# A third group turned by VectorE and the DMA queue, and four sums in an earlier step

## The chip, the cores and the metric

The kernel runs on one core of a Trainium2 chip. The core has TensorE (PE: matrix products and transposes through an identity), VectorE (DVE), ScalarE (ACT), GpSimd (POOL) and SyncE (SP), whose queue issues most of the DMA transfers. Each engine takes its instructions in order and waits on semaphores for the others. The metric is the device time of one execution in microseconds. Before the change the median of three executions is 694.56 us (694.55 to 695.29).

## The reference

The input `u` is a sequence of 2048 rows with 512 channels. The first half of the work, A, is a state-space convolution with a skip term; the second, B, is a mixer with two MLPs.

```
h   = u + A(layernorm(u))
x   = layernorm(h)
g   = gelu(layernorm(x) @ w1)                  # 512 -> 512, layer 1
x1  = x + shifted(g) @ w2                      # four channel quarters shifted by +1, -1, +2, -2 rows; layer 2
h2  = gelu(layernorm(x1) @ w3) @ w4            # 512 -> 1792 -> 512, layers 3 and 4
out = h + x1 + h2
```

All is float32. The products of B are made from split operands: each operand is written as a high part (fp32r) and the rest (low part), and three products of them are summed.

## The kernel before

The convolution (`conv_phase`) takes the first 300 us and is not touched. `mixer_phase` works on the 2048 rows as sixteen tiles of 128 rows, in four groups `q` of four tiles; the order of the groups is 3, 0, 1, 2. For each group `norm1(q)` writes the normalized rows into one of four large tiles `XQ[0]` to `XQ[3]` (128x2048); group 2 uses `XQ[0]`. `turn1(q)` makes the transposed operand `XT[q]` of layer 1: sixteen TensorE transposes of 128x128 into four PSUM banks, then for each of four chunks of channels a cast on ScalarE (high part) and a subtraction on VectorE (low part). `layer1(q, f)` is twelve matmuls of 128x512 for each quarter `f` of the outputs, and a gelu on ScalarE with a low part on VectorE. `layer2(j)` is twelve matmuls for one tile, whose result VectorE adds to the residual into the tile `X1[q]`; for tiles below 8 GpSimd adds it to `h` and VectorE takes the statistics for the second norm.

The products of layers 1 to 4 share four PSUM banks in rotation (pool `ps2`, rows named `l` or `l3a` to `l3g` in the profile), so a matmul group has to wait until the group four places earlier has been read.

Layer 3 is done for two halves of the rows (pair 0 and pair 1), each in seven steps, so that `s` runs from 0 to 13; a step makes seven products with operand sums in the manner of Strassen's scheme. Its operands are the turned tiles of `x1` (`FT[q, c]`), their sums t1 to t4 (`sums2`), and the high and low parts of them all (`halve`; `fresh` for pair 1). In a step, `layer3a` makes the products a, b, c and e, with VectorE adding them up; then comes the fourth layer of the step before (`layer4a`), then `layer3b` with f, d, g and the gelus, then `layer4b`. `turn2(q)` turns a group of `x1` without TensorE: VectorE transposes 32x32 blocks of the whole tile into a second `XQ` tile, four instructions in all, and sixteen DMA transfers of 32x512 from SP's queue put the blocks in their places.

The list `todo` holds small pieces of work, and `some(n)` issues the next `n` of them at the place in the program where it is called; `some(4)` stands at the end of each step.

The order of instructions on each engine is the order in which the code is written; `InOrder` keeps it, and every instruction made through it has line 87 in the profile, so groups of instructions are told apart by the names of their tiles. The order around the change is the list of calls in lines 1424 to 1431 and the loop over `s` from line 1543:

```
    norm1(2), sum3(), layer1(1, 0), layer1(1, 1), layer1(1, 2), turn1(2), layer1(1, 3), load3(0), raw3(1)
    layer2(2), layer2(3), norm2(0), layer2(4), layer2(5)
    layer1(2, 0), turn2(0), layer1(2, 1), load4(0), raw4(1), layer1(2, 2), sum3(), layer1(2, 3), layer2(6)
...
        if s == 4:
            turn2(3)
        if s == 5:
            todo.extend(sums2(1, 0) + sums2(1, 1)), some(4)
```

`raw3` and `raw4` issue the loads of the next weights on SP, `sum3` adds weight quarters on GpSimd, `load3` and `load4` split the weights on ScalarE and GpSimd, and `norm2(q)` normalizes a group of `x1` in place.

Of the kernel before, what the change touches and what calls it, by code (L numbers as in the profile page):

```python
# [11 lines left out]
F32 = mybir.dt.float32  # L12
# [3 lines left out]
ALU = mybir.AluOpType  # L16
# [1112 lines left out]
def mixer_phase(ctx, tc, cst, h, out, finish, w3, w4):  # L1129

    nc = InOrder(tc)
# [10 lines left out]
    def slab(name):  # L1142
        return sl.tile([128, 512], F32R, tag="slab", name=name)

    def slot(i):
        return cst["slab"](i)
# [4 lines left out]
    XQ = [w1p.tile([128, 4 * 512], F32, name=f"xq{i}") for i in range(4)]  # L1151
    X1 = {0: XQ[3], 1: XQ[1], 2: XQ[2], 3: XQ[0]}
    quarter = lambda t, i: t[:, i * 512 : i * 512 + 512]
    turned = lambda t: t.rearrange("p (a c x) -> p c a x", a=4, c=4)
    natural = lambda t: t.rearrange("p (i a t) -> p i a t", i=4, a=4)
# [56 lines left out]
    H1, XL, XT = {}, {}, {}  # L1212

    def norm1(q):
        XL[q] = []
        for j in range(q * 4, q * 4 + 4):
            t = quarter(XQ[{3: 0, 0: 1, 1: 2, 2: 0}[q]], j % 4)
            if (q == 0 and j % 2) or (q == 3 and j != 14):
                nc.vector.tensor_scalar(t, h[:, j, :], mv[:, j, 0:1], r12[:, j : j + 1], ALU.subtract, ALU.mult)
            else:  # L1220
                nc.scalar.activation(t, h[:, j, :], AF.Identity, scale=r12[:, j : j + 1], bias=off12[:, j : j + 1])
            XL[q].append(t)

    def turn1(q):
        XT[q] = transposed(XL.pop(q), f"xt{q}", 2 if q == 3 else 0)

    def layer1(q, f):
        b = bank(f"l1_{q}_{f}")
        n = 0
        seq = [(c, wi, xi) for c in range(4) for wi, xi in PROD]  # L1230
        if (q, f) == (3, 0):

            seq.sort(key=lambda k: 2 * k[0] + 3 * k[2])
        for c, wi, xi in seq:
            nc.tensor.matmul(b, W1[f][wi][:, c * 128 : c * 128 + 128], XT[q][c][xi], start=(n == 0), stop=(n == 11))
            n += 1
        H1[q, f] = gelu(b, f"h1_{q}_{f}")

        tiles = {0: ((15, 0),), 2: ((14, 1), (15, 2)), 1: ((0, 3),), 3: ((0, 4), (1, 5))}[f]
        for t, i in tiles:  # L1240
            if t // 4 != q:
                continue
            for k in range(2):
                src = H1[q, f][k][:, t % 4 * 128 : t % 4 * 128 + 128]
                dst = wrap[k][i // 4][:, i % 4, :]
                if f in (0, 2):
                    nc.gpsimd.tensor_copy(dst[:, 32:128], src[:, 0:96].bitcast(F32))
                    nc.gpsimd.tensor_copy(dst[:, 1:32], src[:, 96:127].bitcast(F32))
                    nc.gpsimd.tensor_copy(dst[:, 0:1], zero)
                else:  # L1250
                    nc.gpsimd.tensor_copy(dst[:, 0:96], src[:, 32:128].bitcast(F32))
                    nc.gpsimd.tensor_copy(dst[:, 96:127], src[:, 1:32].bitcast(F32))
                    nc.gpsimd.tensor_copy(dst[:, 127:128], zero)
# [11 lines left out]
    def layer2(j):  # L1265
        q, i = divmod(j, 4)
        b = bank(f"l2_{j}")
        n = 0
        for f, sh in enumerate((-1, 1, -2, 2)):
            for wi, xi in PROD:  # L1270
                nc.tensor.matmul(b, h1_block(f, j + sh, xi), W2[f][wi], start=(n == 0), stop=(n == 11))
                n += 1
        x1 = quarter(X1[q], i)
        nc.vector.scalar_tensor_tensor(x1, h[:, j, :], r1[:, j : j + 1], b, ALU.mult, ALU.add)
        xq[j] = x1
        if j < 8:
            residual(j), stats2(j)
# [27 lines left out]
    def norm2(q):  # L1305
        for op in norm2_ops(q):
            op()
# [4 lines left out]
    FT, XC, W3, W4 = {}, {}, {}, {}  # L1312

    def turn2(q):

        x, t = X1[q], XQ[{0: 2, 2: 3, 3: 1}[q]]
        blocks = t.rearrange("p (b c i t) -> p i c b t", b=4, c=4, i=4)
        for i in range(4):
            nc.vector.transpose(blocks[:, i], quarter(x, i).rearrange("p (c b t) -> p c b t", c=4, b=4))
        for a in range(4):  # L1320
            for b in range(4):
                nc.sync.dma_start(quarter(x, a)[b * 32 : b * 32 + 32], quarter(t, b)[a * 32 : a * 32 + 32])
        for c in range(4):
            FT[q, c] = turned(x)[:, c]

    def turn2_wide(q):

# [11 lines left out]

    def halve(src, pair, name, c, low=nc.vector):  # L1340

        hi, lo = slab(f"{name}{pair}{c}h"), slab(f"{name}{pair}{c}l")
        src = src.rearrange("p a (i t) -> p i a t", i=4)
        nc.scalar.copy(natural(hi), src)
        low.tensor_tensor(natural(lo), src, natural(hi).bitcast(F32), ALU.subtract)
        XC[pair, name, c] = hi, lo

    def sums2(pair, c):

# [11 lines left out]
    todo = []  # L1361

    def some(n):
        while n and todo:
            todo.pop(0)()
            n -= 1
# [5 lines left out]
    def raw3(s):  # L1372
        f = s % half
        for i in range(2):
            o = (f + i * half) * 128
            nc.sync.dma_start(raw["ab"[i]].rearrange("p (c f) -> p c f", c=4),
                              w3[:, o : o + 128].rearrange("(c p) f -> p c f", p=128))

    def sum3():
        a11, a12, a21, a22 = (raw[n][:, i * 256 : i * 256 + 256] for n in "ab" for i in range(2))  # L1380
        s1, s2, s3, s4 = (raw["s"][:, i * 256 : i * 256 + 256] for i in range(4))
        nc.gpsimd.tensor_tensor(s1, a21, a22, ALU.add)
        nc.gpsimd.tensor_tensor(s3, a11, a21, ALU.subtract)
        nc.gpsimd.tensor_tensor(s2, s1, a11, ALU.subtract)
        nc.gpsimd.tensor_tensor(s4, a12, s2, ALU.subtract)

    def load3(s, low=nc.gpsimd, parts=range(3)):
        ra, a22, sm_ = raw["a"], raw["b"][:, 256:512], raw["s"]
        if s % 2:
            one, four, last = (slot(11), slot(14)), (slots(9, 2), slots(12, 2)), slot(8)  # L1390
        else:
            one, four, last = (slot(20), W3S[0]), (slots(16, 2), slots(18, 2)), W3S[1]
        for i, (src, (hi, lo)) in enumerate(((ra, one), (sm_, four), (a22, (last[:, 0:256], last[:, 256:512])))):
            if i not in parts:
                continue
            nc.scalar.copy(hi, src)
            low.tensor_tensor(lo, src, hi.bitcast(F32), ALU.subtract)
        at_ = lambda w, i: w[:, i * 256 : i * 256 + 256]
        W3[s] = dict(a11=[at_(w, 0) for w in one], a12=[at_(w, 1) for w in one], a22=[at_(last, i) for i in range(2)],
                     **{f"s{i + 1}": [at_(w, i) for w in four] for i in range(4)})  # L1400
# [23 lines left out]
    norm1(3), finish(0, early), turn1(3), gelus(), finish(0, late), root([0]), norm1(0)  # L1424
    layer1(3, 0), layer1(3, 1), layer1(3, 2), turn1(0), finish(1), root([1]), layer1(3, 3), norm1(1), raw3(0), raw4(0)
    finish(2, early), layer1(0, 0), layer1(0, 1), layer1(0, 2), layer1(0, 3), turn1(1), finish(2, late), root([2]), layer2(0), layer2(1)
    norm1(2), sum3(), layer1(1, 0), layer1(1, 1), layer1(1, 2), turn1(2), layer1(1, 3), load3(0), raw3(1)
    layer2(2), layer2(3), norm2(0), layer2(4), layer2(5)
    layer1(2, 0), turn2(0), layer1(2, 1), load4(0), raw4(1), layer1(2, 2), sum3(), layer1(2, 3), layer2(6)
    layer2(7), norm2(1)  # L1430
    for n in ("b11", "b21"):
# [111 lines left out]
    for s in range(2 * half):  # L1543
        turn, last = s + 1 == half, s + 1 == 2 * half
        layer3a(s)
        if turn:
            fresh(("b11", "t2", "t3", "t1"))
        if last:
            load4(s)
        else:  # L1550
            load3(s + 1, *((nc.gpsimd,) if s else (nc.vector, range(1, 3))))
        if s + 2 < 2 * half:
            raw3(s + 2)
        if s:
            layer4a(s - 1)
        if s == 1:
            for j in range(8, 12):
                residual(j), stats2(j)
        if s == 2:
            for j in range(12, 16):  # L1560
                stats2(j)
            norm2(2)
            for j in range(12, 16):
                residual(j)
        if s == 3:
            turn2(2), norm2(3)
        if s == 4:
            turn2(3)
        if s == 5:
            todo.extend(sums2(1, 0) + sums2(1, 1)), some(4)  # L1570
        late = layer3b(s)
        if not last and s:
            load4(s), raw4(s + 1)
        if s + 2 < 2 * half:
            sum3()
        if s:
            layer4b(s - 1, late)
        else:
            late()
        some(4)  # L1580
        if turn:
            fresh(("b21", "t4", "b22"))
# [45 lines left out]
```

## Time and profile before

| | |
|---|---|
| median of three runs | 694.56 us (694.55 to 695.29) |
| the profiled execution | 695.48 us |
| its span, first to last instruction | 693.4 us |
| mean granted TensorE clock | 0.995 |
| TensorE matmul busy | 656.0 us, 95% of the span |
| VectorE, ScalarE, GpSimd busy | 538.6, 411.2, 397.8 us |

A row of the timeline gives the start, the duration, the engine, the line, the operation, the tile written and the tiles read with their shapes, the number of instructions merged into the row, and in brackets the idle time before it and what ended that. Buffer numbers are left out of the names: `l` is any PSUM bank of layers 1, 2 and 4, `u` any of a step's four accumulators, `xt` the PSUM banks of the transposes. Matmuls are pipelined: the next one starts before the end that a row gives.

### The profile page before, as it was taken

Reading aid. Unit: us, or ns where it says so; the run is one execution under the profiler, and the core shown is the slowest. Engines: PE = TensorE matmul, PEld = TensorE weight load, DVE = VectorE, ACT = ScalarE, POOL = GpSimd, SP = SyncE. Lnnn points to the kernel's source line nnn. Section 1 sums busy time; section 2 is a strip of 40 time slices with the busy share of each in tenths; the row PEclk is TensorE's granted clock in tenths of the full one; section 3 lists DMA queues with packets and bytes.
Section 4 is the critical chain, followed back from the end, with each engine's and each line's share of the span. In section 5 each row is a group of like instructions: output and inputs, shape, how many; then the busy total and the mean of one; then the engine's idle time right before and its main releaser. Section 6 shows DMA issues by size and latency. Waiting matters only on the chain.

```text
span 693.4 us, 16766 instructions
## 1 busy us (share of the span) xinstructions
PE 656.0 (95%) x6854; PEld 511.8 (74%) x6854; DVE 538.6 (78%) x946; ACT 411.2 (59%) x712; POOL 397.8 (57%) x406
## 2 busy tenths in 40 slices
PE   5887999998999998989999999999999999999997
PEld 5884756663676674848888888888887888888886
DVE  5998998999898998987776799766679954554544
ACT  7889878867799974236643455445445543444330
POOL 1889589967999998002555309455534655553310
PEclk9998999999999999999999999999999999999999
DMA  8830654010301132010012011223411352211004
GB/s 216 258 140 2 186 160 102 3 48 32 64 2 49 34 108 93 2 61 1 1 32 72 20 30 32 61 83 99 114 40 31 105 140 61 61 46 45 17 15 122
DMA packets 47216, 48.34 MB, mean 70 GB/s; under 512 B 5668, under 2 KB 32292, under 8 KB 47140
## 3 DMA queue, kind: packets, MB, share of 16 engines
q1 hardware_dynamic: 46372, 46.22, 23.2%
q10 hardware_dynamic: 768, 1.05, 0.6%
q8 instruction: 54, 0.88, 0.5%
q14 instruction: 22, 0.18, 0.1%
HBM read 35.72 MB, written 8.39 MB: 64 GB/s over the span
## 4 chain that ended last, share of the span: by engine, by line
PE 58%; DVE 19%; ACT 12%; issue 4%; POOL 4%; DMA 2%; SPq 1%; DVEq 0%; ACTq 0%; POOLq 0%
PE l L87 24%; PE acc L87 10%; ACT pt L87 7%; PE bank L87 6%; DVE u L87 5%; DVE at L87 3%; DVE cs L87 3%; DVE sn L87 3%; PE l3c L87 3%; PE l3f L87 3%; PE l3e L87 3%; PE l3a L87 2%; PE l3b L87 2%; PE l3g L87 2%; PE l3d L87 2%
## 5 line engine op out<-in xcount | busy, mean ns | idle before, releaser
L87 ACT ACTIVATE pt<-pt 128x1056 f32<-128x1056 int32 x64 | 69.9, 1092 | 14.3 <-DVE cs L87 6.6
L87 POOL TENSOR_TENSOR pt<-p,s 128x512 int32<-128x512 int32 x64 | 72.0, 1143 | 5.1 <-DVE sn L87 4.1
L87 PE MATMUL bank<-at,tbs 128*64 128x128 f32 (+1 forms) x768 | 63.1, 311 | 3.4 <-DVE u L87 1.6
L87 PEld LDWEIGHTS bank<-at,tbs 128*64 128x64 f32 x768 | 44.5, 134 | 20.8 <-ACT at L87 3.0
L87 PEld LDWEIGHTS bank<-ident 128*128 128x128 f32 x418 | 50.5, 198 | 8.3 <-issue 5.1
L87 PE MATMUL bank<-ident 128*128 128x128 f32 x418 | 54.6, 287 | 0.0
L87 PE MATMUL bank<-u,ms 64*128 64x128 f32 x768 | 50.5, 280 | 3.5 <-DVE at L87 1.3
L87 PEld LDWEIGHTS bank<-u,ms 64*128 64x128 f32 x768 | 45.3, 187 | 8.2 <-issue 1.8
L87 POOL TENSOR_TENSOR cs0w<-raw,cs0w 128x512 fp32r<-128x512 f32 x7 | 9.4, 1346 | 62.4 <-ACT cs0w L87 50.1
L87 DVE TENSOR_TENSOR cs<-pt,amx 128x512 f32<-128x512 f32 x64 | 40.9, 677 | 2.5 <-ACT pt L87 1.3
L87 DVE TENSOR_TENSOR h<-h,l 128x512 f32<-128x512 f32 x48 | 32.3, 686 | 12.0 <-PE l L87 12.0
L87 DVE TENSOR_TENSOR u<-u,l3f 128x512 f32<-128x512 f32 x14 | 9.6, 686 | 40.5 <-PE l3f L87 40.5
L87 PEld LDWEIGHTS bank<-cs 128*32 128x32 f32 x1024 | 24.1, 111 | 23.0 <-POOL cs L87 6.0
L87 PE MATMUL bank<-cs 128*32 128x64 f32 x1024 | 32.4, 224 | 9.1 <-DVE cs L87 4.8
L87 POOL TENSOR_TENSOR cs1w<-raw,cs1w 128x512 fp32r<-128x512 f32 x7 | 9.5, 1362 | 52.9 <-ACT cs1w L87 39.5
L87 ACT COPY at<-bank 128x512 f32<-128x512 f32 x40 | 24.9, 630 | 22.9 <-PE bank L87 22.8
L87 ACT ACTIVATE pt<-pt,halfpi 128x1056 f32<-128x1056 f32 x32 | 38.1, 1191 | 0.5
L87 POOL TENSOR_TENSOR sn<-pt,amp 128x512 f32<-128x512 f32 x30 | 36.9, 1229 | 1.4 <-ACT pt L87 1.0
L87 DVE STREAM_TRANSPOSE at<-bank 128x512 f32<-128x512 f32 (+1 forms) x40 | 35.6, 919 | 1.5 <-PE bank L87 1.5
L87 ACT ACTIVATE u<-u 128x512 f32<-128x512 f32 x56 | 35.4, 633 | 1.8
L87 PE MATMUL bank<-sn 128*32 128x64 f32 x1024 | 31.9, 222 | 2.6 <-DVE sn L87 2.5
L87 POOL TENSOR_TENSOR cs<-pt,amp 128x512 f32<-128x512 f32 x26 | 31.9, 1227 | 3.4 <-PE bank L87 1.1
(1163 smaller groups left out, 2080.6 us busy)
## 6 DMA issues: line engine op xcount, KB each, us to landing
raw<-in_B_w_dram SPq DMA_DIRECT2D x28, 256.0 KB, 2.7
h<-in_A_u_dram SPq DMA_DIRECT2D x32, 128.0 KB, 4.2
h<-in_A_u_dram SPq DMA_DIRECT2D x16, 256.0 KB, 4.1
rawa<-in_B_w_dram SPq DMA_DIRECT2D x14, 256.0 KB, 2.9
rawb<-in_B_w_dram SPq DMA_DIRECT2D x14, 256.0 KB, 2.7
ms<-in_mm_dram SPq DMA_DIRECT2D x4, 768.0 KB, 11.1
xq<-xq SPq DMA_DIRECT2D x48, 64.0 KB, 2.0
out_dram<-h SPq DMA_DIRECT2D x48, 64.0 KB, 1.7
```

Of the source, the lines that this page charges most:

```text
L87: ins = f(*args, **kw)
```

## The change

The code of `turn2` becomes a function `swap(x, t)`, and that of `halve` a function `parts(src, name, low)`; `turn2` and `halve` call them and do what they did. New is that `turn1(2)` is gone. In its place `swap(XQ[0], XQ[1])` is called right after `norm1(2)` and `sum3()`, ahead of `layer1(1, 0)`, and the four chunks are split by `parts` after `layer2(3)`, ahead of `norm2(0)`. Operand sums of pair 1: the first four, `sums2(1, 0)`, are put on the list in step 4 and so are issued at its end; the other four, `sums2(1, 1)`, are issued in the middle of step 5, where the first four were.

```diff
+    def swap(x, t):
+
+        blocks = t.rearrange("p (b c i t) -> p i c b t", b=4, c=4, i=4)
+        for i in range(4):
+            nc.vector.transpose(blocks[:, i], quarter(x, i).rearrange("p (c b t) -> p c b t", c=4, b=4))
+        for a in range(4):
+            for b in range(4):
+                nc.sync.dma_start(quarter(x, a)[b * 32 : b * 32 + 32], quarter(t, b)[a * 32 : a * 32 + 32])
+        return [turned(x)[:, c] for c in range(4)]
+
+    def parts(src, name, low=nc.vector):
+
+        hi, lo = slab(f"{name}h"), slab(f"{name}l")
+        src = src.rearrange("p a (i t) -> p i a t", i=4)
+        nc.scalar.copy(natural(hi), src)
+        low.tensor_tensor(natural(lo), src, natural(hi).bitcast(F32), ALU.subtract)
+        return hi, lo
...
-    norm1(2), sum3(), layer1(1, 0), layer1(1, 1), layer1(1, 2), turn1(2), layer1(1, 3), load3(0), raw3(1)
-    layer2(2), layer2(3), norm2(0), layer2(4), layer2(5)
+    norm1(2), sum3()
+    third = swap(XQ[0], XQ[1])
+    layer1(1, 0), layer1(1, 1), layer1(1, 2), layer1(1, 3), load3(0), raw3(1)
+    layer2(2), layer2(3)
+    XT[2] = [parts(v, f"xt2{c}") for c, v in enumerate(third)]
+    norm2(0), layer2(4), layer2(5)
...
         if s == 4:
-            turn2(3)
+            turn2(3), todo.extend(sums2(1, 0))
         if s == 5:
-            todo.extend(sums2(1, 0) + sums2(1, 1)), some(4)
+            todo.extend(sums2(1, 1)), some(4)
```

What stands on TensorE between the third and the last quarter of group 1's first layer, before (`xt2_0` to `xt2_3` are the PSUM banks of the transposes, `xq0` is `XQ[0]`):

```order
L87 MATMUL l1_1_2_4419<-xt13l_4317,cs1w_3641 128x512
L87 MATMUL l1_1_2_4419<-xt13h_4316,cs1w_3641 128x512
L87 MATMUL xt2_0_4438<-ident_61,xq0_3948 128x128 x4
L87 MATMUL xt2_1_4439<-ident_61,xq0_3948 128x128 x4
L87 MATMUL xt2_2_4440<-ident_61,xq0_3948 128x128 x4
L87 MATMUL xt2_3_4441<-ident_61,xq0_3948 128x128 x4
L87 MATMUL l1_1_3_4474<-xt10h_4292,sn0w_3588 128x512
```

And after; the last quarter follows at once:

```order
L87 MATMUL l1_1_2_4439<-xt13l_4317,cs1w_3641 128x512
L87 MATMUL l1_1_2_4439<-xt13h_4316,cs1w_3641 128x512
L87 MATMUL l1_1_3_4458<-xt10h_4292,sn0w_3588 128x512
L87 MATMUL l1_1_3_4458<-xt10l_4293,sn0w_3588 128x512
L87 MATMUL l1_1_3_4458<-xt10h_4292,sn0w_3588 128x512
```

On VectorE at the same place, before (`h1_1_0l` to `h1_1_3l` are low parts of group 1's gelus, `xt20l` to `xt23l` those of the turned third group):

```order
L87 BN_AGGR mv2_0_4351<-st1_1_4370 128x2
L87 TENSOR_TENSOR h1_1_0l_4395<-gh1_1_0_4396,h1_1_0h_4394 128x512
L87 TENSOR_TENSOR h1_1_1l_4414<-gh1_1_1_4415,h1_1_1h_4413 128x512
L87 TENSOR_TENSOR h1_1_2l_4433<-gh1_1_2_4434,h1_1_2h_4432 128x512
L87 TENSOR_TENSOR xt20l_4447<-xt2_0_4438,xt20h_4446 128x512
L87 TENSOR_TENSOR xt21l_4455<-xt2_1_4439,xt21h_4454 128x512
L87 TENSOR_TENSOR xt22l_4463<-xt2_2_4440,xt22h_4462 128x512
L87 TENSOR_TENSOR xt23l_4471<-xt2_3_4441,xt23h_4470 128x512
L87 TENSOR_TENSOR h1_1_3l_4488<-gh1_1_3_4489,h1_1_3h_4487 128x512
L87 SCALAR_TENSOR_TENSOR xq3_3951<-h_66,rr_67,l2_2_4501 128x512
```

And after, where the block transposes stand ahead of the gelus' low parts, and those of the third group (not in these rows) behind the sums and statistics of `layer2(2)` and `layer2(3)`, with `XQ[0]` as their source:

```order
L87 BN_AGGR mv2_0_4351<-st1_1_4370 128x2
L87 STREAM_TRANSPOSE xq1_3949<-xq0_3948 128x4x4x32 x4
L87 TENSOR_TENSOR h1_1_0l_4415<-gh1_1_0_4416,h1_1_0h_4414 128x512
L87 TENSOR_TENSOR h1_1_1l_4434<-gh1_1_1_4435,h1_1_1h_4433 128x512
L87 TENSOR_TENSOR h1_1_2l_4453<-gh1_1_2_4454,h1_1_2h_4452 128x512
L87 TENSOR_TENSOR h1_1_3l_4472<-gh1_1_3_4473,h1_1_3h_4471 128x512
L87 SCALAR_TENSOR_TENSOR xq3_3951<-h_66,rr_67,l2_2_4485 128x512
```

The casts of the third group move in the same way on ScalarE, behind the weights of `load3(0)` and ahead of `norm2(0)`. On SP the sixteen transfers stand ahead of `raw3(1)`.

On VectorE from the end of step 4 into step 5, before (`u_5` are step 5's accumulators, `xq` the tiles that hold the operands and sums of pair 1):

```order
L87 TENSOR_TENSOR h<-h,l_3_3_5779 128x512
L87 TENSOR_TENSOR u_5_5788<-u_5_5787,l3b_5799 128x512
L87 TENSOR_TENSOR u_5_5789<-u_5_5788,l3c_5807 128x512
L87 TENSOR_TENSOR u_5_5790<-u_5_5789,l3e_5815 128x512
L87 TENSOR_TENSOR u_5_5788<-u_5_5788,l3e_5815 128x512
L87 TENSOR_TENSOR xq_3951<-xq_3948,xq_3950 128x512
L87 TENSOR_TENSOR xq_3948<-xq_3948 128x4x128
L87 TENSOR_TENSOR xq_3951<-xq_3948,xq_3951 128x512
L87 TENSOR_TENSOR xq_3951<-xq_3950,xq_3951 128x512
L87 TENSOR_TENSOR u_5_5787<-u_5_5787,l3f_5864 128x512
```

And after; the same four sums stand ahead of the first addition of step 5, and the four of the second chunk (into `xq_3949`) where these were. At the end of step 5 no sum is left:

```order
L87 TENSOR_TENSOR h<-h,l_3_3_5779 128x512
L87 TENSOR_TENSOR xq_3951<-xq_3948,xq_3950 128x512
L87 TENSOR_TENSOR xq_3948<-xq_3948 128x4x128
L87 TENSOR_TENSOR xq_3951<-xq_3948,xq_3951 128x512
L87 TENSOR_TENSOR xq_3951<-xq_3950,xq_3951 128x512
L87 TENSOR_TENSOR u_5_5792<-u_5_5791,l3b_5803 128x512
L87 TENSOR_TENSOR u_5_5793<-u_5_5792,l3c_5811 128x512
L87 TENSOR_TENSOR u_5_5794<-u_5_5793,l3e_5819 128x512
L87 TENSOR_TENSOR u_5_5792<-u_5_5792,l3e_5819 128x512
L87 TENSOR_TENSOR xq_3949<-xq_3948,xq_3950 128x512
```

More of the change, by code (lines that the diff above doesn't have):

```diff
@@ L1314, in turn2 @@
     def turn2(q):
[L1316 to L1324, printed above, removed]
+        for c, v in enumerate(swap(X1[q], XQ[{0: 2, 2: 3, 3: 1}[q]])):
+            FT[q, c] = v
     def turn2_wide(q):
@@ L1340, in halve @@
     def halve(src, pair, name, c, low=nc.vector):
[L1342 to L1346, printed above, removed]
+        XC[pair, name, c] = parts(src, f"{name}{pair}{c}", low)
     def sums2(pair, c):
```

## The prediction

> **What bounds the kernel now.** I read the page's busy shares first, then the stretches around the two places that the change touches, then TensorE's waits in them, then the single instructions there.
>
> ```profile
> PE 656.0 (95%) x6854; PEld 511.8 (74%) x6854; DVE 538.6 (78%) x946; ACT 411.2 (59%) x712; POOL 397.8 (57%) x406
> ```
>
> The share is an average, so the stretches matter more (from:to, length, then busy time of PE, PEld, DVE, ACT, POOL, PE clock, DMA):
>
> ```profile
> 342.00:373.00 31.00, 31.00 (x147) 25.85 (x146) 20.23 (x40) 15.91 (x30) 18.27 (x15) 1.00 0.10 26
> 373.00:513.00 140.00, 139.93 (x623) 115.22 (x622) 103.28 (x187) 67.89 (x113) 65.78 (x59) 1.00 0.22 63
> 513.00:532.00 19.00, 18.54 (x82) 15.04 (x81) 18.05 (x21) 8.68 (x16) 9.92 (x8) 1.00 0.18 56
> 532.00:689.20 157.20, 157.20 (x694) 129.78 (x692) 90.46 (x131) 64.78 (x108) 65.89 (x58) 1.00 0.23 64
> ```
>
> From 342 us to the last matmul TensorE is busy without a break at clock 1.00, but for about half a microsecond before 532. The table of waits has one line for it in that time:
>
> ```profile
> PE l L87 <- DVE u L87: 0.5, 1, 0.5
> ```
>
> So in the whole second phase a microsecond taken from TensorE's queue is a microsecond of the kernel, as long as nobody else becomes late. Work on VectorE, ScalarE and the queues costs nothing until TensorE has to wait for it.
>
> **First part: the transposes of the third group.** TensorE's rows there:
>
> ```profile
> 346.22 0.40 PE L87 MATMUL l<-xt13h,cs1w 128*128 128x512 f32 x1
> 346.45 1.91 PE L87 MATMUL xt<-ident,xq 128*128 128x128 f32 x16
> ...
> 348.43 0.39 PE L87 MATMUL l<-xt10l,sn0w 128*128 128x512 f32 x1
> ...
> 361.87 0.39 PE L87 MATMUL l<-xt20h,cs0w 128*128 128x512 f32 x1
> ```
>
> A row's length is longer than its turn: the step from 346.22 to 346.45 shows that one wide matmul takes 0.23 us of the queue. Without the sixteen transposes the first matmul of layer1(1, 3) starts at 346.45 and the second at 346.68, where now it starts at 348.43: 1.75 us gained. Everything behind moves up by that, so layer1(2, 0), which first needs the third group, wants it at 361.87 - 1.75 = 360.1.
>
> What must be ready then takes a long way round. Its links, on ScalarE, VectorE, the DMA queue and ScalarE again (the 366 and 369 rows are the same swap of group 0, which this kernel already does, and the last two give the pitch of a cast from such a tile):
>
> ```profile
> 339.78 2.94 ACT L87 ACTIVATE xq<-h,rn,rr 128x512 f32<-128x512 f32 x4 [4.95 <-DVE rn L87]
> ```
> ```profile
> 342.74 0.18 DVE L87 BATCH_NORM_AGGREGATE mv<-st 128x2 f32<-128x6 f32 x1
> ...
> 347.77 0.69 DVE L87 TENSOR_TENSOR h_2l<-gh,h_2h 128x512 fp32r<-128x512 f32 x1 [2.03 <-ACT gh L87]
> ...
> 358.36 0.17 DVE L87 TENSOR_SCALAR qa<-mv 128x4 f32<-128x4 f32 x1
> ...
> 361.40 0.74 DVE L87 SCALAR_TENSOR_TENSOR xq<-h,rr,l 128x512 f32<-128x512 f32 x1
> ...
> 366.59 2.48 DVE L87 STREAM_TRANSPOSE xq<-xq 128x512 f32<-128x512 f32 x4
> ```
> ```profile
> 369.15 10.14 SPq L1322 DMA_DIRECT2D xq<-xq  x16
> ```
> ```profile
> DMA to landing us min/median/max: 1.9/2.0/2.6
> ```
> ```profile
> 385.06 0.61 ACT L87 CAST b1100h<-xq 128x512 fp32r<-128x512 f32 x1
> 385.57 0.61 ACT L87 CAST b1101h<-xq 128x512 fp32r<-128x512 f32 x1
> ```
>
> The normalized group is written by 339.78 + 2.94 = 342.7 and VectorE is free at 342.74 + 0.18 = 342.9. Four block transposes take 2.48: 345.4. SP has nothing else in front of the sixteen transfers; their issue takes 10.14, from 345.5 to 355.6, the last one starting at about 355.0 and landing 2.0 to 2.6 later: 357.0 to 357.6. Every chunk of the turned tile takes rows from all quarters, so ScalarE's first cast waits for the last transfer. Four casts at a pitch of 0.51 run from 357.1; the first is done at 357.7. The first VectorE subtraction then ends at about 358.4, and with a pitch of 0.60 (the rows of t1 in the chain below) the fourth at 360.3.
>
> TensorE wants the first high part at 360.1 (slack 2.4 us), the first low part one matmul later at 360.3 (slack 1.9), the fourth low part ten matmuls later at 362.4 (slack 2.1). So by these rows the whole detour is hidden, and a slip above 1.9 us starts to cost TensorE one for one.
>
> What stands behind the moved instructions: VectorE is held 2.5 us more before the low parts of layer1(1, 0) and (1, 1), which then run from 345.4 to 346.7; the third, at 347.77, is not touched. ScalarE and VectorE both wait at the third group until 357 to 358; behind them are norm2(0) and, on VectorE, the residual sum of layer2(4). From the start of norm2(0) to that sum it is now 361.40 - 358.36 = 3.0 us; from 360.3 the sum ends at 364.1. It frees the PSUM bank (four rotate) that layer1(2, 2) takes 24 matmuls after layer1(2, 0), at 360.1 + 5.4 = 365.5: 1.4 us to spare. The swap of group 0 starts some 0.5 us later than now, and its 16 transfers land near 382, against the first cast of it at 385.06 - 1.75 = 383.3. The next weight loads on SP are issued from 355.6 on; GpSimd's sums that read them come at 372.01 - 1.75 (row below). I take the first part as 1.75 gained; the bounds are 1.75 and, if all slacks are lost, what the rivals below give.
>
> **Second part: the four sums.** The chain of waits, from the end of the fifth step (start, us, what):
>
> ```profile
> 515.05 0.98 DVE xq L87
> ...
> 516.05 2.28 DVE xq L87 x2
> ...
> 518.98 0.67 DVE u L87
> ...
> 520.53 1.29 DVE u L87 x2
> 521.82 1.67 DVE b1110l L87
> 523.49 2.81 DVE b1111l L87
> ...
> 529.85 0.60 DVE t111l L87
> 530.45 0.61 DVE u L87
> ```
>
> TensorE's rows at both ends of it:
>
> ```profile
> 519.37 0.39 PE L87 MATMUL l3e<-t101h,ptw 128*128 128x512 f32 x1
> ...
> 530.25 0.39 PE L87 MATMUL l<-sn0w,h_511h 128*128 128x512 f32 x1
> 531.10 0.50 PE L87 MATMUL l<-cs1w,h_501h 128*128 128x512 f32 x1 [0.46 <-DVE u L87]
> 531.44 0.40 PE L87 MATMUL l<-cs1w,h_501l 128*128 128x512 f32 x1
> ```
>
> This is the kernel's one wait after 342 us. The second four sums (515.05 to 516.05 + 2.28 = 518.3) push the additions of the sixth step's products, these the eight low parts, and these the addition at 530.45 that frees the bank. The row says 0.46, but by the steps TensorE loses (531.10 - 530.25 - 0.23) + (531.44 - 531.10 - 0.23) = 0.62 + 0.11 = 0.73. With those sums gone from this place the last two additions wait only for product e, whose last matmul ends at 519.37 + 0.39 = 519.76: they start at 519.8 instead of 520.53, 0.73 earlier, and the chain behind releases the bank at about 530.3, before TensorE asks at 530.48. That is 0.15 to spare, so the gain is between 0.4 and 0.73; I take 0.7. Below zero it cannot go here, since nothing is added to this chain.
>
> The sums come back one half step earlier, each: the first four now stand at the end of the fourth step, right after the swap of the fourth group. DMA queue, then VectorE:
>
> ```profile
> 483.74 10.01 SPq L1322 DMA_DIRECT2D xq<-xq  x16
> ```
> ```profile
> 493.96 0.69 DVE L87 TENSOR_TENSOR h<-h,l 128x512 f32<-128x512 f32 x1 [0.67 <-PE l L87]
> 496.74 0.69 DVE L87 TENSOR_TENSOR u<-u,l3b 128x512 f32<-128x512 f32 x1 [2.09 <-PE l3b L87]
> ...
> 506.20 0.69 DVE L87 TENSOR_TENSOR u<-u,l3f 128x512 f32<-128x512 f32 x1 [2.69 <-PE l3f L87]
> ```
>
> The transfers land (483.74 + 10.01 - 0.63 = 493.1 is the last issue) 493.1 + 2.0 to 2.6, at 495.1 to 495.7; VectorE would be free at 494.6 and waits about a microsecond. Four sums as slow as those above (3.3 us) end at 499.0, so the addition at 496.74 slips by 2.3 us and the last of the step's first additions ends near 501.6; the second four sums then end by 505, before 506.20. Nothing of TensorE's hangs on it earlier: cost nothing.
>
> **Sum.** 1.75 + 0.7 = 2.45 us. The profiled execution took 695.48 (span 693.4) and would become 693.0; the median of the three runs is 0.92 below it, and 694.56 - 2.45 = 692.1 is my number. 0.2%, 1.39 us here, is about what a measurement can tell from no change.
>
> **Rivals.** *VectorE held by GpSimd.* The four low parts now read two SBUF tiles, where one operand came from PSUM. In the chain above two such low parts took 1.67 and 2.81 instead of 0.60. What GpSimd does at the time, and a swap's transposes beside GpSimd:
>
> ```profile
> 357.13 2.55 POOL L87 TENSOR_TENSOR h<-h,xq 128x512 f32<-128x512 f32 x2
> ...
> 372.01 1.19 POOL L87 TENSOR_TENSOR raws<-rawb 128x256 f32<-128x256 f32 x1
> ...
> 480.12 2.42 POOL L87 TENSOR_TENSOR amp0w<-raws,sn1w 128x1024 fp32r<-128x1024 f32 x1
> ```
> ```profile
> 480.20 2.48 DVE L87 STREAM_TRANSPOSE xq<-xq 128x512 f32<-128x512 f32 x4
> ```
>
> The transposes keep their 2.48 beside a GpSimd instruction. GpSimd's two residuals move up to 355.4 and end at 357.9, when the low parts begin, and the next one needs layer2(4)'s sum; so little is shared. Were all four to take 1.67, the fourth would end at 357.7 + 4 x 1.67 = 364.4, 2.0 after it is wanted: the gain would shrink to 0.45, 694.1.
>
> [...]
>
> *The swap lands late (slower).* From 1.9 us of slip on, TensorE waits one for one; at 4.35 us the gain is eaten. That needs issues of 0.90 instead of 0.63 us. An end 2 us beyond that gives 696.6. Against it: the two swaps shown took 10.01 and 10.14, and at that time SP carries nothing else.
>
> *The wait moves instead of going.* VectorE is busy for 18.05 of the 19 us from 513 on; if its low parts merely stretch against GpSimd, the 0.73 stays: 692.8.
>
> *Nothing comes of it:* the banks or norm2(0) give back what the transposes free, about 694.4.
>
> [...]
>
> **Chances.** Forecast 0.60, the wait that stays 0.10, GpSimd 0.10, nothing 0.09, late swap 0.11. Forecast, the staying wait and half of the GpSimd cases (a partial overlap) are faster by over 0.2%: 0.75. The rest of GpSimd and nothing: 0.14 the same. Slower: 0.11. The range reaches down to 694.56 - 2.48 - 0.4 (half the spread of the runs, 694.55 to 695.29) = 691.7 and up to 694.3, which takes in most of the GpSimd cases.
>
> **What would show it.** Right: layer1(1, 3) follows layer1(1, 2) without a gap; layer1(2, 0) starts near 360.1 with no idle time before it; the first cast of the third group starts near 357; TensorE's one wait on VectorE is gone. Wrong: idle time of TensorE before the first matmuls of layer1(2, 0), released by ScalarE or VectorE; transfers spaced over 0.7 us; a wait of layer1(2, 2) for a bank; a new wait near 500.

## The result, and the profile after

| | before | after |
|---|---|---|
| median | 694.89 us (6 runs, 694.38 to 695.29) | 691.67 us (6 runs, 691.56 to 692.73) |
| ratio after / before, 95% interval | | 0.9958 [0.9947, 0.9968] |
| profiled execution (its span) | 695.48 us (693.4) | 691.70 us (689.8) |

The ratio is a gain of 2.9 us, between 2.2 and 3.7. The kernel became faster, and 691.67 lies in the range and 0.4 us under the predicted 692.1.

The two profiled executions differ by 3.6 us of span, more than the change made. The first phase, which the change does not touch, took 0.92 us less in the second: the last matmul of layer1(1, 2), the last one ahead of the change on TensorE, started at 346.22 before and at 345.30 after. In these two traces the difference arises near the start of the kernel: from 17.5 to 29.1 us the matmuls of both stand within 0.01 us of each other, then TensorE waits for VectorE 1.21 us before its matmul at 30.73 (before) and 0.24 us before the one at 29.76 (after). Over the profiled executions of all kernels below that start lies anywhere between 345.22 and 346.54. So I measure the length from this matmul to the last matmul of the kernel, which leaves the first phase out:

| kernel | start of the last matmul of layer1(1, 2) | start of the last matmul | length, us | against before |
|---|---|---|---|---|
| before | 346.22 | 688.82 | 342.60 | |
| after | 345.30 | 685.28 | 339.98 | -2.62 |
| after, a second profile | 345.40 | 685.35 | 339.95 | -2.65 |
| e1_turn_only | 345.48 | 686.12 | 340.64 | -1.96 |
| e2_sums_only | 345.33 | 687.12 | 341.79 | -0.81 |
| e3_three_ahead | 345.47 | 687.27 | 341.80 | -0.80 |
| e4_eight_ahead | 345.57 | 690.66 | 345.09 | +2.49 |
| e5_gpsimd_beside | 345.37 | 690.64 | 345.27 | +2.67 |
| e6_split_ahead | 345.22 | 688.68 | 343.46 | +0.86 |
| e7_group_one_too | 345.74 | 686.22 | 340.48 | -2.12 |
| e8_group_one_sorted | 346.54 | 686.24 | 339.70 | -2.90 |

The two profiles of the changed kernel agree within 0.03 us by this measure.

The busy shares of after, from the page; sixteen TensorE instructions are gone:

```profile
PE 654.2 (95%) x6838; PEld 510.7 (74%) x6838; DVE 542.3 (79%) x950; ACT 410.8 (60%) x712; POOL 398.7 (58%) x406
```

The stretches of after that answer to those of before (from:to, length, then busy time of PE, PEld, DVE, ACT, POOL, PE clock, DMA):

```profile
342.00:370.30 28.30, 28.30 (x127) 23.41 (x126) 20.99 (x43) 15.04 (x28) 16.47 (x15) 1.00 0.24 65
370.30:510.20 139.90, 139.84 (x624) 115.21 (x622) 109.58 (x191) 67.73 (x113) 67.07 (x58) 1.00 0.22 63
510.20:529.00 18.80, 18.80 (x84) 15.48 (x83) 14.80 (x19) 9.11 (x17) 10.64 (x9) 1.00 0.20 57
529.00:685.60 156.60, 156.60 (x691) 129.39 (x690) 90.07 (x130) 64.26 (x107) 65.82 (x58) 1.00 0.23 64
```

In the stretch from 510 TensorE is now busy for all of it, and VectorE, which was busy for 18.05 us of 19, for 14.80 of 18.80: the sums have left it. The table of TensorE's waits from 300 us on has one line left, in the first group's transposes at the start of the phase, and none on VectorE:

```profile
PE xt L87 <- ACT h L87: 1.0, 1, 1.0
```

TensorE's rows of after at the two places:

```profile
345.30 0.39 PE L87 MATMUL l<-xt13h,cs1w 128*128 128x512 f32 x1
345.52 0.39 PE L87 MATMUL l<-xt10h,sn0w 128*128 128x512 f32 x1
345.75 0.39 PE L87 MATMUL l<-xt10l,sn0w 128*128 128x512 f32 x1
...
359.15 0.39 PE L87 MATMUL l<-xt20h,cs0w 128*128 128x512 f32 x1
359.38 0.39 PE L87 MATMUL l<-xt20l,cs0w 128*128 128x512 f32 x1
...
372.36 0.50 PE L87 MATMUL l<-amp0w,h_3l 128*128 128x512 f32 x1
...
527.42 0.39 PE L87 MATMUL l<-sn0w,h_511h 128*128 128x512 f32 x1
527.65 0.42 PE L87 MATMUL l<-cs1w,h_501h 128*128 128x512 f32 x1
527.91 0.39 PE L87 MATMUL l<-cs1w,h_501l 128*128 128x512 f32 x1
```

Layer1(1, 3) follows layer1(1, 2) in 0.22 us. Its second matmul moved from 348.43 to 345.75, 2.68 earlier; without the 0.92 of the first phase that is **1.76 us**, the sixteen transposes. Layer1(2, 0) starts 2.72 earlier: nothing is lost on the way, and 0.04 more is gained over the matmuls between. In layer2(6), at the low part `h_3l`, before lost 0.17 and 0.11 us and after 0.06 and 0.11. At 527 the 0.62 and 0.11 us that were lost ahead of `h_501` are down to about 0.03: from 530.25 to 527.42 the matmul ahead of it moved by 2.83, the one two behind it (531.44 to 527.91) by 3.53, which is **0.70 us**. So 1.76 + 0.04 + 0.11 + 0.70 = 2.61 of the 2.62.

The detour of the third group in after, on VectorE, SP and ScalarE:

```profile
341.96 2.46 DVE L87 STREAM_TRANSPOSE xq<-xq 128x512 f32<-128x512 f32 x4
...
356.87 0.69 DVE L87 TENSOR_TENSOR xt20l<-xq,xt20h 128x512 fp32r<-128x512 f32 x1 [1.26 <-ACT xt20h L87]
...
358.68 0.68 DVE L87 TENSOR_TENSOR xt23l<-xq,xt23h 128x512 fp32r<-128x512 f32 x1
...
371.35 0.95 DVE L87 TENSOR_TENSOR h_3l<-gh,h_3h 128x512 fp32r<-128x512 f32 x1 [0.19 <-ACT gh L87]
```
```profile
344.50 10.13 SPq L1234 DMA_DIRECT2D xq<-xq  x16
```
```profile
356.21 0.62 ACT L87 CAST xt20h<-xq 128x512 fp32r<-128x512 f32 x1 [4.92 <-DMA xq<-xq]
```

The first cast stands at 356.21 (predicted 357.1, and 356.2 with the 0.92 taken off), the last low part ends at 359.36, and TensorE wants the first low part at 359.38, where it is ready since 357.56.

### The profile page after: what moved, and what is told of

Its sections match the earlier page's. It is cut to its first block, busy times and chain, and to the rows that moved or that the text cites. A ratio compares the mean times of both kernels' runs of the same rounds, so it can differ in the third digit from the quotient of the medians.

```text
span 689.8 us, 16757 instructions
## 1 busy us (share of the span) xinstructions
PE 654.2 (95%) x6838; PEld 510.7 (74%) x6838; DVE 542.3 (79%) x950; ACT 410.8 (60%) x712; POOL 398.7 (58%) x406
## 4 chain that ended last, share of the span: by engine, by line
PE 61%; DVE 15%; ACT 15%; POOL 4%; issue 4%; DMA 0%; SPq 0%; ACTq 0%; DVEq 0%; POOLq 0%
PE l L87 24%; PE acc L87 11%; ACT pt L87 8%; PE bank L87 7%; DVE u L87 4%; PE l3c L87 3%; PE l3f L87 3%; PE l3e L87 3%; DVE at L87 3%; PE l3a L87 3%; PE l3b L87 3%; PE l3d L87 3%; PE l3g L87 3%; DVE cs L87 2%; DVE sn L87 2%
```

## The experiments

**The two parts apart.** `e1_turn_only` has the third group's way round and the sums where they were:

```diff
         if s == 4:
-            turn2(3), todo.extend(sums2(1, 0))
+            turn2(3)
         if s == 5:
-            todo.extend(sums2(1, 1)), some(4)
+            todo.extend(sums2(1, 0) + sums2(1, 1)), some(4)
```

> The third group's turn by VectorE and the queue alone; the eight sums stand where they stood before the change. My theory: TensorE gains 1.75 us by the sixteen transposes that are gone, nothing more, and its wait of about half a microsecond on VectorE in the sixth step is back (0.73 us by the steps of its matmuls). So 1.75 to 1.9 us faster than before the change, and 0.7 to 0.9 slower than the whole change. The rival, that the turn brought all of the 2.9 us and the sums nothing, expects the time of the whole change.

Measured: 693.27 us, ratio to before 0.9981 [0.9970, 0.9992], length -1.96: the 1.76 of the transposes, and 0.17 that before lost ahead of `h_3l` and this kernel does not. The wait at the end of step 5 is back. TensorE's rows there, where 0.62 and 0.10 us are lost, as in before:

```profile
527.57 0.39 PE L87 MATMUL l<-sn0w,h_511h 128*128 128x512 f32 x1
528.42 0.50 PE L87 MATMUL l<-cs1w,h_501h 128*128 128x512 f32 x1 [0.46 <-DVE u L87]
528.75 0.39 PE L87 MATMUL l<-cs1w,h_501l 128*128 128x512 f32 x1
```

`e2_sums_only` is the kernel before with only the sums moved:

```diff
         if s == 4:
-            turn2(3)
+            turn2(3), todo.extend(sums2(1, 0))
         if s == 5:
-            todo.extend(sums2(1, 0) + sums2(1, 1)), some(4)
+            todo.extend(sums2(1, 1)), some(4)
```

> The sums alone, half a step earlier each; the third group is turned by TensorE as before the change. My theory: the one wait of TensorE in the sixth step goes and nothing else changes, 0.7 us faster than before. The rival, that the wait only moves to another place, expects no difference to the kernel before, with a new idle time of TensorE on VectorE between 495 and 545 us.

Measured: 694.80 us, ratio 0.9992 [0.9983, 1.0001], length -0.81; the timing alone cannot tell it from no change, the trace can: TensorE's wait on `u` is gone and no other came. The two parts add up: 1.96 + 0.81 = 2.77, against 2.62 with both.

**How much the swap may slip.** `e3_three_ahead` and `e4_eight_ahead` let SP issue three or eight further transfers of the same kind ahead of the sixteen, into a tile that is written anew before anyone reads it:

```diff
-    def swap(x, t):
+    def swap(x, t, ahead=0):
...
+        for n in range(ahead):
+            a, b = n // 4, n % 4
+            nc.sync.dma_start(quarter(XQ[2], a)[b * 32 : b * 32 + 32], quarter(t, b)[a * 32 : a * 32 + 32])
...
-    third = swap(XQ[0], XQ[1])
+    third = swap(XQ[0], XQ[1], 3)
```

(with 8 in its place in the other).

> The whole change, with three extra transfers of the same size on SP's queue ahead of the sixteen (into a tile that is free then; they serve nothing). Each issue takes 0.63 us, so the last landing slips by 1.9 us, which is the slack that the trace of the changed kernel shows before the first low part (it ends at 357.6, wanted at 359.4). My theory: no idle time of TensorE, or below 0.2 us, and the time of the whole change. The rival, that the detour is on the path already and only its gain is larger, expects 1.9 us more.

Measured: 694.39 us, ratio 0.9992 [0.9983, 1.0001], length 1.82 more than after. The expected time of the whole change did not come; the 1.9 us of the rival nearly did, but not at the place where I had put the limit: at layer1(2, 0) TensorE lost 0.07 and 0.11 us, as I expected. The table of waits has a line that after has not:

```profile
PE l L87 <- DVE h_3l L87: 1.5, 1, 1.5
```

By the steps 1.64 and 0.11 us are lost there, in layer2(6). VectorE's rows of this kernel show the way from the late low parts to it:

```profile
358.88 0.69 DVE L87 TENSOR_TENSOR xt20l<-xq,xt20h 128x512 fp32r<-128x512 f32 x1 [3.10 <-ACT xt20h L87]
...
361.30 0.17 DVE L87 TENSOR_SCALAR qa<-mv 128x4 f32<-128x4 f32 x1
...
367.48 0.69 DVE L87 TENSOR_TENSOR h_0l<-gh,h_0h 128x512 fp32r<-128x512 f32 x1 [0.85 <-ACT gh L87]
368.09 2.48 DVE L87 STREAM_TRANSPOSE xq<-xq 128x512 f32<-128x512 f32 x4
370.49 1.53 DVE L87 TENSOR_TENSOR h_1l<-gh,h_1h 128x512 fp32r<-128x512 f32 x1
...
373.09 1.21 DVE L87 TENSOR_TENSOR h_3l<-gh,h_3h 128x512 fp32r<-128x512 f32 x1
```

The low parts start 2.01 us later than in after, 1.84 of it slip and 0.17 the longer first phase. Norm2(0) behind them is as late (361.30), then the gelu of layer1(2, 0) on ScalarE, whose low part is `h_0l`; the swap of group 0 and three low parts follow without a gap, the latter at 1.21 to 1.53 us instead of 0.69 (in after 1.53, 1.23 and 0.95, where GpSimd's splits and sums run beside them from 366.91 to 373.72). `h_3l` starts at 373.09 instead of 371.35. In after the same row has an idle time of 0.19 us in front of it, and that is no reserve here: `h_3l` takes 1.21 us instead of 0.95, and TensorE waited 0.06 us for it in after already. Of a slip of 1.84 us the kernel pays 1.82.

> The same with eight extra transfers ahead: the last landing slips by 5.0 us, 3.1 to 3.2 beyond the slack. My theory: TensorE waits 3.2 us at the start of the third group's first layer, released by the low part, and the kernel takes 3.2 to 3.4 us more than the whole change, about the time before the change or a little over. The rival, that something else behind the cast (norm2 of group 0 or a bank) sets in earlier, expects more than 3.6.

Measured: 697.24 us, ratio 1.0039 [1.0026, 1.0052], length 5.11 more than after, well above the 3.2 to 3.4 that I took for likely. TensorE waited 2.82 us at layer1(2, 0) and 0.49 at its second matmul. These 3.3 us are what I expected. What I did not expect stands behind them. TensorE's rows and the stretch from there (columns as above, PE clock third from the end):

```profile
362.25 0.51 PE L87 MATMUL l<-xt20h,cs0w 128*128 128x512 f32 x1 [2.66 <-ACT xt20h L87]
362.97 0.55 PE L87 MATMUL l<-xt20l,cs0w 128*128 128x512 f32 x1 [0.22 <-DVE xt20l L87]
363.32 0.63 PE L87 MATMUL l<-xt20h,cs0w 128*128 128x512 f32 x1
363.75 0.63 PE L87 MATMUL l<-xt21h,cs0w 128*128 128x512 f32 x1
...
366.72 0.40 PE L87 MATMUL l<-xt23l,cs0w 128*128 128x512 f32 x1
```
```profile
362.20:366.70 4.50, 4.23 (x10) 3.13 (x11) 4.13 (x15) 1.55 (x3) 0.00 (x0) 0.62 0.29 86
```

The granted clock is 0.62 over 4.5 us, and the matmuls come at a pitch of 0.43 instead of 0.23: nine steps lost 1.7 us more. But the wait at `h_3l` is almost gone (0.09), and VectorE has 0.17 us idle ahead of that row: TensorE and VectorE now come to it together. So the slow clock took the place of a wait that VectorE's late queue would have caused, as in `e3_three_ahead`, and as far as this run shows it added nothing: a slip of 5.09 us (5.36 less 0.27 of the first phase) cost 5.11. The rival, norm2(0) behind the cast with more than 3.6, is what came. Slips below 1.84 us were not run.

**GpSimd beside the low parts.** `e5_gpsimd_beside` adds five additions of 128x512 on GpSimd at the time of the four low parts (in a tile that the next `sum3` overwrites unread):

```diff
     layer2(2), layer2(3)
+    for i in range(5):
+        nc.gpsimd.tensor_tensor(raw["s"][:, 0:512], raw["s"][:, 0:512], raw["s"][:, 512:1024], ALU.add)
     XT[2] = [parts(v, f"xt2{c}") for c, v in enumerate(third)]
```

> The whole change, with five additions of 128x512 on GpSimd, both operands in SBUF, put behind its two residuals, so that they run while VectorE makes the four low parts of the third group (356.9 to 359.4 us); they add up scratch numbers that nobody needs. The rival of the prediction, that VectorE is held by GpSimd: the low parts take 1.2 to 1.7 us instead of 0.69, the fourth ends 2 to 4 us later, against a slack of 2.1, and the kernel takes 0 to 2 us more. Were there no contention, the low parts keep 0.69 and the time is that of the whole change.

Measured: 698.34 us, ratio 1.0042 [1.0030, 1.0055], length 5.29 more than after, where I expected 0 to 2. VectorE's rows, and GpSimd's:

```profile
356.96 0.69 DVE L87 TENSOR_TENSOR xt20l<-xq,xt20h 128x512 fp32r<-128x512 f32 x1 [1.26 <-ACT xt20h L87]
357.57 1.79 DVE L87 TENSOR_TENSOR xt21l<-xq,xt21h 128x512 fp32r<-128x512 f32 x1
359.28 1.77 DVE L87 TENSOR_TENSOR xt22l<-xq,xt22h 128x512 fp32r<-128x512 f32 x1
360.98 1.77 DVE L87 TENSOR_TENSOR xt23l<-xq,xt23h 128x512 fp32r<-128x512 f32 x1
362.67 1.25 DVE L87 TENSOR_SCALAR qa<-mv 128x4 f32<-128x4 f32 x1
...
364.16 1.14 DVE L87 TENSOR_SCALAR qr<-qb 128x4 int32<-128x4 int32 x1
```
```profile
356.98 8.30 POOL L87 TENSOR_TENSOR raws<-raws 128x512 f32<-128x512 f32 x5
```

Three low parts take 1.77 to 1.79 instead of 0.69, and GpSimd's additions 8.30 / 5 = 1.66 each instead of 1.28 to 1.30 (the residuals of after). The last two rows are small steps of norm2(0), which take 0.16 and 0.17 in after. TensorE loses 1.37 us before the low parts of layer1(2, 0), 1.58 at the bank of layer1(2, 2), and 2.43 at `h_3l`: 5.4 in all. So both engines took longer side by side here, and the 5.29 would have eaten the gain of 2.62 twice over. In after GpSimd's two residuals end at 356.97, as the next row says, the first low part starts at 356.87, and the four take 0.68 to 0.69:

```profile
354.41 2.56 POOL L87 TENSOR_TENSOR h<-h,xq 128x512 f32<-128x512 f32 x2
```

**Where the split stands.** `e6_split_ahead` puts the four casts and low parts ahead of layer2(2) in the code, so that on VectorE they stand ahead of the residual sums of tiles 2 and 3:

```diff
-    layer2(2), layer2(3)
     XT[2] = [parts(v, f"xt2{c}") for c, v in enumerate(third)]
+    layer2(2), layer2(3)
```

> The whole change, with the split of the third group put ahead of layer2(2) and layer2(3) instead of behind them, so that VectorE waits for the transfers with the sums of these two tiles behind it in its queue. My theory: the swap itself is no later, but the sum of layer2(2), which frees a PSUM bank for the third group's first layer, runs only after the fourth low part: at 359.4 + 0.75 = 360.1 instead of 351.9, and TensorE, which wants the bank at 359.15, waits about 1 us there; the sums of layer2(3) to (5) and norm2(0) come late in turn, for another 0 to 2 us. So 1 to 3 us slower than the whole change. If the place in the queue did not matter, the time would be the same.

Measured: 696.92 us, ratio 1.0025 [1.0014, 1.0036], length 3.48 more than after, a little above the expected 1 to 3. The profiled execution, 695.11, is the fastest of eleven, so the length is that of the fastest. Its table of waits:

```profile
PE l L87 <- DVE h_3l L87: 2.1, 1, 2.1
...
PE l L87 <- DVE xq L87: 0.8, 1, 0.8
```

VectorE now stands idle for 6.6 us before the first low part, with work behind it. The sums it holds up free a bank 1.0 us late, and norm2(0) starts later, which is paid at `h_3l` again. So the place behind layer2(3), where VectorE has nothing else to do while the transfers fly, is what hides the detour.

These four runs make the third group or norm2(0) late in three ways, and one number tells the price of each: when VectorE ends the small steps of norm2(0), on which ScalarE's normalization of the group waits (tile `qo`), counted from the start of the last matmul of layer1(1, 2).

| kernel | small steps of norm2(0) end, us | later than after | length more than after |
|---|---|---|---|
| after | 16.13 | | |
| e3_three_ahead | 17.97 | 1.84 | 1.82 |
| e6_split_ahead | 19.67 | 3.54 | 3.48 |
| e4_eight_ahead | 21.22 | 5.09 | 5.11 |
| e5_gpsimd_beside | 21.51 | 5.38 | 5.29 |

Whatever delayed norm2(0), the kernel paid the delay one for one to within 0.1 us, wherever TensorE happened to wait.

**A second group in the same way.** Of `x1`, group 1 still goes through TensorE in 16 transposes (`turn2_wide(1)`). `e7_group_one_too` turns it with `swap` too, issued by SP and ScalarE in turn, and takes the operand sums of pair 0 behind layer2(12) in the order in which layer 3 needs them:

```diff
-    def swap(x, t):
+    def swap(x, t, queues=(nc.sync,)):
...
-                nc.sync.dma_start(quarter(x, a)[b * 32 : b * 32 + 32], quarter(t, b)[a * 32 : a * 32 + 32])
+                queues[b % len(queues)].dma_start(quarter(x, a)[b * 32 : b * 32 + 32], quarter(t, b)[a * 32 : a * 32 + 32])
...
-    layer2(8), layer2(9), layer2(10), turn2_wide(1)
-    rest = []
-    for c in range(2):
-        t1, t3, t2, t4 = sums2(0, c)
-        part = lambda n, c=c: lambda: halve(FT[0, "sums", c][n], 0, n, c)
-        todo.extend((t1, part("t1"), t3, t2, part("t2"), part("t3"), t4))
-        rest.extend((part("t4"), part("b22")))
-    for j in range(11, 15):
-        some(3), layer2(j)
-    some(1), layer2(15), some(1)
+    for c, v in enumerate(swap(XQ[1], XQ[0], (nc.sync, nc.scalar))):
+        FT[1, c] = v
+    for j in range(8, 13):
+        layer2(j)
+    ops = [dict(zip(("t1", "t3", "t2", "t4"), sums2(0, c))) for c in range(2)]
+    part = lambda n, c: lambda: halve(FT[0, "sums", c][n], 0, n, c)
+    for n in ("t1", "t3", "t2"):
+        todo.extend([o[n] for o in ops] + [part(n, c) for c in range(2)])
+    todo.extend(o["t4"] for o in ops)
+    rest = [part(n, c) for c in range(2) for n in ("t4", "b22")]
+    some(6), layer2(13), some(4), layer2(14), some(4), layer2(15)
```

> The whole change, and group 1 of x1 also turned by VectorE and transfers instead of sixteen TensorE transposes, with the transfers dealt out to SP's and ScalarE's queues, and the sums of pair 0 made in the order in which step 0 needs them. If two queues issue at 0.63 each side by side, the last transfer lands near 392, the first sum moves from 385.1 to 392, and the products that need the sums (e at 400.2, then every 1.36 us) are just met: TensorE gains another 1.75 us, 689.9. If the issues do not overlap, the last lands at 397, the first product that needs a sum waits 2 to 4 us and the kernel is 1 to 3 us slower than the whole change.

Measured: 693.05 us, ratio 0.9976 [0.9965, 0.9988], length 0.50 more than after; the expected 689.9 did not come. The 1.76 us of the transposes are gained, and about 2.3 given back. VectorE waits for the last transfer (its first sum), and then has no gap until after 413 us, so what comes last in its queue is late; TensorE's longest wait:

```profile
393.02 1.29 DVE L87 TENSOR_TENSOR t<-xq,xq 128x512 f32<-128x512 f32 x2 [2.12 <-DMA xq<-xq]
...
407.21 0.69 DVE L87 TENSOR_TENSOR u<-u,l3b 128x512 f32<-128x512 f32 x1
```
```profile
PE l3g L87 <- DVE u L87: 1.3, 1, 1.3
```

`e8_group_one_sorted` changes that kernel in two places: it deals the transfers ten to six and lets that addition of product b go ahead of a low part and of the low part of the weights, and the addition of c ahead of the latter too:

```diff
-                queues[b % len(queues)].dma_start(quarter(x, a)[b * 32 : b * 32 + 32], quarter(t, b)[a * 32 : a * 32 + 32])
+                queues[b % len(queues) if a < 3 else 0].dma_start(quarter(x, a)[b * 32 : b * 32 + 32], quarter(t, b)[a * 32 : a * 32 + 32])
...
-            for i in (0, 2, 1, 3):
+            for i in (0, 2, 1):
                 rest[i]()
-            load3(1, nc.vector, range(1))
             plus(two, prod(s, "b", "s2", "t2"), one)
+            rest[3]()
             plus(three, c, two)
+            load3(1, nc.vector, range(1))
```

> Group 1 of x1 turned by VectorE and transfers as in e7_group_one_too, but ten transfers are issued by SP and six by ScalarE (there eight and eight), and in the first step of layer 3 the addition that ends product b stands two low parts and the low part of the weights earlier in VectorE's queue. There TensorE gained 1.76 us by the sixteen transposes and lost 0.27 and 0.26 us before products e and b, 1.51 before product g and 0.51 before product c of the next step. Theory, the loss is VectorE's queue, first by the landing of the last transfer and then by the order of its additions: six issues of 0.74 instead of eight bring the last landing from 393.0 to about 391.7, which covers the 0.27 and 0.26; the addition of b starts near 405.4 instead of 407.2 and the 1.51 goes; the 0.51 may stay. Then TensorE loses 0.5 us or less of the 1.76, and the kernel takes 1.2 to 1.7 us less than the changed kernel: 690.0 to 690.5 beside its 691.7. Rival, the amount of VectorE's work between the landing and product g is the limit and the order only shifts the wait: the waits before c and e of the next step grow to 1.5 us or more, and the time is that of e7_group_one_too, about 0.6 us over the changed kernel.

> The changed kernel once more, on the same chip and with as many runs as the others: 691.6 to 692.6, ratio to before 0.9958 within 0.001.

Measured: 692.20 us (691.31 to 692.70), ratio 0.9948 [0.9935, 0.9962], and the changed kernel on the same chip 691.86 us (691.83 to 692.71), 0.9953 [0.9940, 0.9965]. By the times the two cannot be told apart, and the expected 690.0 to 690.5 did not come. By length e8 is 0.25 to 0.28 shorter than the two profiles of after, so most of the 1.76 us is still given back. TensorE's rows of e8 in step 1 with the two waits that it has left behind 400 us:

```profile
411.08 0.50 PE L87 MATMUL l3b<-t200h,amp0w 128*128 128x512 f32 x1 [0.34 <-DVE amp0w L87]
...
412.61 0.50 PE L87 MATMUL l3c<-t300h,sn1w 128*128 128x512 f32 x1 [0.35 <-DVE u L87]
```

The loss before g fell from 1.51 to 0.27 us, and those before products e and b are gone. The first sum behind the last landing starts 0.6 us earlier (393.22, less 0.80 of the first phase, against 393.02), where 1.3 was expected. In step 1 now 0.22 us are lost at product b's first matmuls (410.03) and 0.61 at each of the two rows, where the second profile of the changed kernel loses 0.32. That is the rival in part: the earlier landing and the new order together were worth 0.78 us (the lengths of e7 and e8), and no run parts the two. I put the rest down to the amount of VectorE's work behind a late landing; no run takes some of that work away, so this is not shown.

## Why the prediction was right

**First part, 1.75 us: right.** The trace gives 1.76, and `e1_turn_only` alone 1.96 in length, with 0.17 of it from `h_3l`. The detour came as worked out, to a tenth of a microsecond in these: 10.13 us of issue, first cast at 356.2 and last low part at 359.4 (predicted 360.3 less 0.92 of the first phase). "The swap of group 0 starts some 0.5 us later" was 0.4 (from 366.59 to 366.08, less the 0.92). The sum of layer2(4) ended 1.1 us before the predicted time (362.1 against 364.1 less 0.92): the small steps of norm2(0) took 2.07 us and not 3.0, since in before one of them had taken 1.14 beside GpSimd.

**"A slip above 1.9 us starts to cost TensorE one for one": wrong.** A slip of 1.84 us, below that limit, already cost 1.82, at another place. The prediction followed the low parts to layer1(2, 0), to the bank of layer1(2, 2) and to the swap of group 0, and stopped there; norm2(0), which stands behind the low parts, leads on through ScalarE's gelu and the same queue to `h_3l` of layer2(6), stretched beside GpSimd. The forecast was not hurt because nothing slipped, but that was luck: the room for error was 0.2 us at most. VectorE's rows of before at that place were there to be read:

```profile
365.98 0.69 DVE L87 TENSOR_TENSOR h_0l<-gh,h_0h 128x512 fp32r<-128x512 f32 x1 [1.31 <-ACT gh L87]
...
371.35 1.25 DVE L87 TENSOR_TENSOR h_2l<-gh,h_2h 128x512 fp32r<-128x512 f32 x1 [1.71 <-ACT gh L87]
374.07 1.07 DVE L87 TENSOR_TENSOR h_3l<-gh,h_3h 128x512 fp32r<-128x512 f32 x1 [1.47 <-ACT gh L87]
```

It had 1.31, 1.71 and 1.47 us idle ahead of these low parts, which then waited for ScalarE alone; after has 0.85 ahead of `h_0l`, where it waits for ScalarE's gelu that hangs on the same norm2(0), and 0.19 ahead of `h_3l`. The change used up that reserve. In before TensorE lost 0.17 us there all the same, as `h_3l` took 1.07 us beside GpSimd's sums instead of 0.69.

**Second part, 0.7 us: right.** 0.70 by the steps. The bound "between 0.4 and 0.73" held. "Four sums as slow as those above (3.3 us) end at 499.0 … cost nothing" was too low in size and right in effect. VectorE's rows of after, and what GpSimd does beside them:

```profile
492.55 0.93 DVE L87 TENSOR_TENSOR xq<-xq,xq 128x512 f32<-128x512 f32 x1 [0.73 <-DMA xq<-xq]
...
494.55 4.58 DVE L87 TENSOR_TENSOR xq<-xq,xq 128x512 f32<-128x512 f32 x2
499.06 0.67 DVE L87 TENSOR_TENSOR u<-u,l3b 128x512 f32<-128x512 f32 x1
```
```profile
495.74 2.84 POOL L87 TENSOR_TENSOR ptw<-raws,ptw 128x1024 fp32r<-128x1024 f32 x1
```

From 492.55 to 499.1 they take 6.6 us, twice the 3.3, the last two at 1.78 and 2.77 beside GpSimd's splits of weights (494.04 to 498.58). The queue recovers by 514, and TensorE loses nothing.

**The sum.** 2.45 was predicted, 2.62 is the length's difference and 2.9 [2.2, 3.7] the times'. Of the 0.17 us between the first two, 0.11 is the wait at `h_3l`, which the sum left out. That 691.67 is 0.4 below 692.1 is within the 0.92 us by which executions differ in the first phase.

**The rivals.** GpSimd holding VectorE did not come, for the reason given (GpSimd's residuals are over); `e5_gpsimd_beside` shows it would have cost more than the 2.0 us that I priced, because the small steps of norm2(0) are held too: the fourth low part ends 3.3 us late, norm2(0) 5.38, and that goes on to the bank and to `h_3l`. The late swap did not come; its price was too small, since the cost does not wait for 1.9 us of slip. The break-even of 4.35 us is wrong by that: 1.84 us of slip already left `e3_three_ahead` at 0.9992 of before, and at one for one the 2.62 gained are eaten by a slip of about 2.6 (an estimate from these lengths). That the wait moves instead of going did not come: with the sums away VectorE is busy for 14.80 of 18.80 us there.

## What to carry to other kernels

Where TensorE was full, work taken out of its queue was worth its whole time (1.76 us in after, where the long way round ended before it was wanted); put the waiting instructions of that way at the place where their engines have nothing else to do, since in order a wait held up everything behind it (6.60 us of VectorE in `e6_split_ahead`, whose length is 3.48 more than that of after). To know how much the way may slip, follow each engine's queue past the first consumer, to the next place where TensorE touches what that engine makes, and look for the smallest idle time in the queue (here 0.19 us ahead of `h_3l`) and for a place where TensorE already waits a little (0.06 us there), not for the slack at the nearest deadline (1.9 us). Doing the same again for the next group was not the same gain: by length `e7_group_one_too` took 0.50 us more than after and `e8_group_one_sorted` 0.25 to 0.28 less, where 1.76 was to be had. That the idle time which hid the first one was missing there is my reading; no run shows it.

## What the runs showed of the hardware

In `e4_eight_ahead` a wait of TensorE of 2.82 us, then one matmul and 0.49 us more, was followed by a granted clock of 0.62 over the stretch from 362.20 to 366.70 us, with nine steps of 0.35 to 0.43 us instead of 0.23; it was 1.00 in the stretches on both sides (359.40 to 362.20 and 366.70 to 372.00). Waits of 1.00 and 2.30 us (`e6_split_ahead`), 1.64 (`e3_three_ahead`), and 1.47 and 2.32 (`e5_gpsimd_beside`) left the pitch at 0.23 in these traces. In the first phase, waits of 0.72 us before 258.73 and 1.32 before 261.15 left the clock at 1.00 in after (258.00 to 264.00). How long a wait must be for such a slow stretch, and whether the wait alone brings it, no run shows.

Beside GpSimd a VectorE subtraction of two SBUF tiles took 1.77 to 1.79 us instead of 0.69, and GpSimd's own addition 1.66 instead of 1.28 to 1.30 (`e5_gpsimd_beside`): both engines lost. Other instructions of VectorE beside GpSimd went both ways: the block transposes kept their 2.48 us (before, 480.20, with GpSimd busy for 2.42 from 480.12), but small steps of norm2(0), 128x4, took 1.14 us in before (at 358.56) and 1.25 and 1.14 in `e5_gpsimd_beside`, with one of 0.17 between these two (363.95), and 0.16 to 0.17 in after, where GpSimd is idle from 356.97 to 362.17. Why they differ the traces do not show.
